# An attention and channel-mix kernel: the order of every engine, written out by hand before, made at trace time after

## The chip, the cores and the metric

The kernel runs on one core of one Trainium2 chip. The metric is the device time of one execution in microseconds (us). Before the change three runs gave 718.5, 718.63 and 719.32 us, with a median of 718.63 us.

## The reference

```python
# q, k, v: (8, 8, 576, 64);  x: (8, 576, 512);  w_k: (512, 1024), w_v: (1024, 512), w_r: (512, 512)
scores = scale * q @ k.T                       # scale = 1 / 8
mask   = (rel >= 0) & (rel < 64)               # rel = query position - key position
attn   = softmax(where(mask, scores, -1e9))    # divided by its sum + 1e-9
x      = (attn @ v), heads side by side        # (8, 576, 512)
x_prev = x shifted by one position, zero first
xk = mu_k * x + (1 - mu_k) * x_prev
xr = mu_r * x + (1 - mu_r) * x_prev
k  = maximum(xk @ w_k, 0)
v  = (k * k) @ w_v
r  = sigmoid(xr @ w_r)
out = r * v
```

A sliding-window attention over 64 positions feeds a channel-mix block: two mixes of each position with the one before it, three matrix products, a squared ReLU and a sigmoid gate.

## The kernel before

**Tiling of the attention.** The 576 positions of each batch and pair of heads are cut into 9 blocks of 64 queries; a block sees 128 keys. Eight blocks make a group, and there are 37 groups (the fifth holds four blocks). For one group TensorE (PE) writes the scores into two PSUM banks (`s`, one for each head of the pair; `scores`). For each half h of the group VectorE (DVE) adds the mask and takes the row's least value, four times (`pr`, `nmax`; in `soften`; the order lists it as ISA with a second row for `nmax`, and the profile as CUSTOM_DVE_ANT_0 with a READ_ACCUMULATOR). ScalarE (ACT) takes the exponential with the row's sum, four times. DVE makes the reciprocals (`rs`, `norm`), GpSimd (POOL) multiplies the four tiles by them (`pr<-pr,rs`), PE transposes them into one PSUM bank (`t`, `flip`), and ACT copies that bank out (`pt`, `keep`). With both halves there, PE multiplies with the values (`x`, `values`) and ACT copies the result into the transposed activations (`xT`, `keep_x`).

**Tiling of the channel mix.** The positions are cut into 11 units of 256, 320 and nine times 448 columns (`UNITS`). Every fp32 operand of the big products is split into a high and a low part in the fast fp32r format, so that each product takes three matmuls. For each unit DVE mixes (`d`, in `mix`), ACT rounds to the high part and POOL subtracts for the low part (`xk`, `xr`). Then PE does 96 matmuls with w_k, 48 with w_r and 96 with w_v. Each result tile of w_k goes through ACT (ReLU, `kf`), POOL (square), ACT (high part, `ks`) and DVE (low part, `ks<-kf,ks`); the w_r results go through ACT (`th`, `r`) and DVE; the w_v results are gated by DVE (`r<-m,r`, in the first unit `r<-mv,r`) and stored.

**Weights.** They come as 64-bit floats in 20 pieces of 128 x 512, four of w_r, eight of w_k and eight of w_v, and are decoded on the chip: ACT takes the absolute high word (`wt<-w`), DVE does four operations (`wt<-wt`, `wp<-wt`, `wp<-w,wp`, `wt<-w,wp`), ACT makes the high part (`ws`) and POOL the low part. All 20 are decoded before the first unit is through.

**What sets the order.** The wrapper class `Engine` keeps the compute instructions of each engine in the order in which the Python code issues them, so the order of the trace is the order on the engine; the transfers are issued by SyncE without it. That order is written by hand: a literal prologue for the first two groups, four weight pieces and the first mixes, and then a clock of steps. A step is six matmuls of the unit at work (`STEP = 6`, 40 steps to a unit). `BEGIN` lists the step at which each group's scores go to PE; `later(n, fn)` puts a follow-up n steps on; decodes stand two steps apart; the mixes for the next unit have fixed steps (20 to 39 of a unit). The transposes follow the scores by a number of steps worked out from the distance to the next group. In the first unit the w_v products run over the pieces of w_v in the outer loop, with two banks for all four results (`v_first`, tile `mv`); later units finish one result after another (`v_units`).

**Buffers around it.** `tmp` has five slots, shared by decode words, mixes, ReLU results and `th`; products and decodes share four PSUM banks (`m`); scores have two banks, `t` one, `x` one.

Of the kernel before, what the change touches and what calls it, by code (L numbers as in the profile page):

```python
# [9 lines left out]
F32 = mybir.dt.float32  # L10
# [6 lines left out]
P = 128  # L17
# [32 lines left out]
def attn_rwkv_kernel(ctx, tc, qT, kT, v2, mu_k, mu_r, w_k, w_v, w_r, out):  # L50
# [22 lines left out]
    pe, dve, sca, pool = (Engine(e) for e in (nc.tensor, nc.vector, nc.scalar, nc.gpsimd))  # L73
    now = 0
    due = {}
# [39 lines left out]
    raw = []  # L115

    def load_w(n):

        for ws, w, i, c in chunks[len(raw):len(raw) + n]:
            st = const.tile([P, WC, 2], U32, name="w", tag="w", bufs=len(chunks))  # L120
            nc.sync.dma_start(st.rearrange("p c t -> p (c t)"),
                              w[i * P:(i + 1) * P, c * WC:(c + 1) * WC].bitcast(U32))
            raw.append(st)
# [6 lines left out]
    def dec_abs(n):  # L130
        words[n] = tmp.tile([P, WC], F32, name="wt", tag="tmp", bufs=TB)
        sca.activation(words[n], raw[n][:, :, 1].bitcast(F32), AF.Abs)

    def dec_bits(n):
        lo, hi = raw[n][:, :, 0], raw[n][:, :, 1]
        tf = words[n]

        pt = ps_m.tile([P, WC], U32, name="wp", tag="m")
        dve.tensor_scalar(tf, tf, HI_MIN, HI_MAX, op0=ALU.max, op1=ALU.min)
        dve.tensor_scalar(pt, tf.bitcast(U32), 3, 0x3FFFFFF8,  # L140
                          op0=ALU.logical_shift_left, op1=ALU.bitwise_and)
        dve.scalar_tensor_tensor(pt, hi, 0xC0000000, pt, op0=ALU.bitwise_and, op1=ALU.bitwise_or)
        dve.scalar_tensor_tensor(tf.bitcast(U32), lo, 29, pt,
                                 op0=ALU.logical_shift_right, op1=ALU.bitwise_or)

    def dec_high(n):
        ws, _, i, c = chunks[n]
        ws[i, c] = const.tile([P, 2, WC], F32R, name="ws", tag="w", bufs=len(chunks))
        sca.copy(ws[i, c][:, 0], words[n])
# [436 lines left out]
```

## Time and profile before

| | before |
|---|---|
| median of 3 runs | 718.63 us |
| the profiled execution | 719.05 us |
| span of its profile (first to last instruction) | 716.8 us |
| PE busy | 650.5 us, 91% |
| DVE busy | 444.1 us, 62% |
| ACT busy | 367.2 us, 51% |
| POOL busy | 339.0 us, 47% |
| transfers | 56.5 MB, 79 GB/s over the span |

Times in the profile's rows are microseconds from the start of the span, but "mean ns" is in nanoseconds. A row of the timeline gives start, length, engine, line, operation, output and input tiles, shape and how many were merged; in brackets stands idle time before it and what ended that. A row of the stages table gives, for a stretch of the span, its length and then the busy time of each engine with the number of instructions, the TensorE clock granted, the busy share of the transfer engines and GB/s. All compute is recorded at one line, that of the wrapper (L71 before, L73 after), so groups are told apart by tiles.

### The profile page before, as it was taken

How to read it: one execution, taken by the hardware profiler on the slowest of the kernel's cores; microseconds unless marked ns; L12 is line 12 of the kernel's file. 1: busy time of each engine (PE TensorE's matmuls, PEld its weight loads, DVE VectorE, ACT ScalarE, POOL GpSimd, SP SyncE). 2: the span in 40 equal slices, each digit the busy share in tenths (PEclk: the TensorE clock that was granted, in tenths of full speed). 3: DMA queues.
4: the chain of work that ended last, by engine and by line, in shares of the span. 5: the costliest groups of instructions: out<-in, count | busy, mean ns of one | idle time of the engine just before them, and what ended most of it. 6: DMA issues, size and time to landing. Idle time of an engine off the chain costs nothing.

```text
span 716.8 us, 14398 instructions
## 1 busy us (share of the span) xinstructions
PE 650.5 (91%) x5232; PEld 584.0 (81%) x5232; DVE 444.1 (62%) x1372; ACT 367.2 (51%) x1111; POOL 339.0 (47%) x503
## 2 busy tenths in 40 slices
PE   4547665988999999999999999999999999999997
PEld 2446554887888988988889999988889898999997
DVE  4888887537636944873693584487368548638241
ACT  4556554555466446546635555645574563342330
POOL 4645464453743664454365375445436643424410
PEclk9857877999999999999999999999999999999999
DMA  8960220422221122233211022122221200101001
GB/s 253 339 246 32 88 70 0 156 64 72 91 94 63 60 89 64 76 109 101 81 53 58 14 83 89 63 77 102 70 88 60 89 1 15 39 1 38 14 1 52
DMA packets 33766, 56.50 MB, mean 79 GB/s; under 512 B 5024, under 2 KB 16800, under 8 KB 33696
## 3 DMA queue, kind: packets, MB, share of 16 engines
q1 hardware_dynamic: 33696, 55.59, 23.3%
q8 instruction: 41, 0.67, 0.4%
q14 instruction: 29, 0.24, 0.1%
HBM read 46.14 MB, written 9.44 MB: 78 GB/s over the span
## 4 chain that ended last, share of the span: by engine, by line
PE 74%; DVE 12%; ACT 6%; DMA 4%; issue 2%; SPq 1%; POOL 1%; ACTq 0%; POOLq 0%
PE m L71 59%; PE s L71 5%; PE x L71 4%; PE t L71 4%; DVE d L71 4%; DVE wp L71 3%; DVE wt L71 2%; ACT pr L71 2%; DMA v<-v 2%; DMA w<-w_v 1%; ACT wt L71 1%; DVE pr L71 1%; POOL pr L71 1%; PE mv L71 1%; DVE r L71 1%
## 5 line engine op out<-in xcount | busy, mean ns | idle before, releaser
L71 PE MATMUL m<-xk,ws 128*128 128x448 f32 (+2 forms) x1056 | 215.2, 358 | 4.8 <-POOL ws L71 2.4
L71 POOL TENSOR_SCALAR pr<-pr,rs 128x128 f32<-128x128 f32 x288 | 127.7, 461 | 189.1 <-DVE nmax L71 147.7
L71 PEld LDWEIGHTS m<-xk,ws 128*128 128x128 f32 x1056 | 188.3, 191 | 17.5 <-ACT ws L71 2.6
L71 PE MATMUL m<-ks,ws 128*128 128x448 f32 (+1 forms) x960 | 197.0, 361 | 0.0
L71 PEld LDWEIGHTS m<-ks,ws 128*128 128x128 f32 x960 | 174.4, 188 | 12.0
L71 DVE TENSOR_TENSOR ks<-kf,ks 128x448 fp32r<-128x448 f32 (+2 forms) x88 | 56.3, 640 | 125.9 <-ACT ks L71 125.9
L71 ACT ACTIVATE pr<-pr,nmax 128x128 f32<-128x128 f32 x288 | 112.9, 396 | 41.5 <-DVE nmax L71 41.4
L71 PE MATMUL m<-xr,ws 128*128 128x448 f32 (+2 forms) x528 | 114.5, 368 | 3.7 <-ACT xr L71 1.9
L71 POOL TENSOR_TENSOR kf<-kf 128x448 f32<-128x448 f32 (+2 forms) x88 | 77.9, 885 | 77.8 <-ACT kf L71 77.5
L71 PEld LDWEIGHTS m<-xr,ws 128*128 128x128 f32 x528 | 97.0, 198 | 11.4 <-POOL xr L71 2.7
L71 PE MATMUL t<-ident,pr 128*128 128x128 f32 x288 | 54.3, 302 | 41.4 <-ACT pt L71 26.3
L71 PEld LDWEIGHTS t<-ident,pr 128*128 128x128 f32 x288 | 37.7, 150 | 56.8 <-POOL pr L71 25.4
L71 ACT CAST ks<-kf 128x448 fp32r<-128x448 f32 (+2 forms) x88 | 47.5, 540 | 66.6 <-POOL kf L71 66.4
L71 DVE TENSOR_TENSOR d<-xT 128x256 f32<-128x256 f32 (+6 forms) x136 | 78.2, 575 | 0.1
L71 DVE CUSTOM_DVE_ANT_0 pr<-s,maskNone 128x128 f32<-128x128 f32 x224 | 55.2, 283 | 28.1 <-PE s L71 28.0
L71 POOL TENSOR_TENSOR xr<-d,xr 128x448 fp32r<-128x448 f32 (+2 forms) x44 | 51.2, 1170 | 32.0 <-ACT xr L71 31.7
L71 POOL TENSOR_TENSOR xk<-d,xk 128x448 fp32r<-128x448 f32 (+2 forms) x44 | 54.8, 1255 | 23.6 <-ACT xk L71 23.6
L71 ACT ACTIVATION_READ_ACCUMULATOR pr<-pr,nmax 128x1 f32 x288 | 54.9, 191 | 0.0
L71 ACT COPY xT<-x 128x256 f32<-128x256 f32 (+7 forms) x68 | 23.2, 391 | 59.7 <-PE x L71 59.6
L71 ACT COPY pt<-t 128x512 f32<-128x512 f32 (+1 forms) x74 | 42.2, 570 | 20.3 <-PE t L71 19.8
L71 PE MATMUL s<-k,q 64*64 64x128 f32 x1152 | 46.1, 302 | 5.9 <-DMA q<-qT 5.9
L71 DVE SCALAR_TENSOR_TENSOR d<-d,mur,xT 128x256 f32<-128x256 f32 (+6 forms) x68 | 49.1, 722 | 2.4
(44 smaller groups left out, 611.7 us busy)
## 6 DMA issues: line engine op xcount, KB each, us to landing
v<-v SPq DMA_DIRECT2D x56, 256.0 KB, 4.2
k<-kT SPq DMA_DIRECT2D x28, 288.0 KB, 2.8
q<-qT SPq DMA_DIRECT2D x28, 288.0 KB, 3.7
w<-w_k SPq DMA_DIRECT2D x8, 512.0 KB, 6.4
w<-w_v SPq DMA_DIRECT2D x8, 512.0 KB, 10.4
outT<-r SPq DMA_DIRECT2D x12, 224.0 KB, 1.9
w<-w_r SPq DMA_DIRECT2D x4, 512.0 KB, 4.6
outT<-r SPq DMA_DIRECT2D x12, 160.0 KB, 1.8
```

The lines of the kernel that those rows point to most:

```text
L71: return lambda *args, **kw: tc.keep_in_program_order(op(*args, **kw))
```

## The change

The clock of steps, `later`, `step`, the prologue and `at_step` go. Every piece of work becomes a `Piece` with an engine, a key (the step at which the hand-written order had it), an estimated length in ns, the pieces that it needs, and the buffers (`Hold`) that it takes or uses. `play` plays all pieces through on paper, when the kernel is traced: whenever an engine is free it takes, of its pieces whose inputs are there and whose buffers are free, the one with the lowest key. The list of pieces in the order in which they began is then traced, and as every engine keeps that order, so does the chip; the transfers are now kept in it too. A decode becomes seven pieces, so that other work may come between DVE's four operations. A product becomes pieces of three matmuls, so that several results may be open at once, and the first unit's w_v products now take the form of the later ones, with `spare=1` to leave a bank for the decodes. All eight maxima of a group may now precede the first reciprocals. The amount of work on every engine is unchanged, and so are the buffers, except that the small `sums` tiles have eight slots in place of four.

```diff
-BEGIN = (0, 6, 12, 18, 26, 34, 43, *range(53, 184, 10),
+BEGIN = (-30, -29, 0, 6, 12, 18, 26, 34, 43, *range(53, 184, 10),
          196, 210, 223, 236, 250, 263, 277, 286, 295, 304, 312, 322, 332, 342, 352)
+LINK = 50
...
-    def later(steps, fn, *args):
-        due.setdefault(now + steps, []).append((fn, args))
-
-    def step():
-        nonlocal now
-        now += 1
-        for fn, args in due.pop(now, ()):
-            fn(*args)
+    pe, dve, sca, pool, dma = (Engine(e) for e in (nc.tensor, nc.vector, nc.scalar, nc.gpsimd, nc.sync))
+    room = {"tmp": TB, "m": 4, "s": 2, "t": 1, "x": 1, "pr": 3, "sums": 4, "pt": 2, "xT": XB,
+            "ks": 8, "r": R_BUFS, "xr": 1, "xk": 1, "qk": 2, "v": 3}
...
+    def play():
+
+        left, free, now, begun = {}, {}, 0, []
+        for n, p in enumerate(pieces):
+            left.setdefault(p.engine, []).append((p.key, n, p))
+            free[p.engine] = 0
+        for e in left:
+            left[e].sort(key=lambda x: x[:2])
...
+            for e, ps in left.items():
+                if free[e] > now:
+                    continue
+                for i, (_, n, p) in enumerate(ps):
+                    if not all(q.done is not None and q.done + (q.lag if q.engine != e else 0) <= now
+                               for q in p.needs):
+                        continue
+                    tags = [h.tag for h in p.takes]
+                    if any(room[tag] < tags.count(tag) + p.spare for tag in set(tags)):
+                        continue
+                    del ps[i]
+                    for tag in tags:
+                        room[tag] -= 1
+                    free[e] = now + p.cost
+                    p.done = free[e]
+                    begun.append(p)
...
+    def over(n):
+
+        return 75 + 1.15 * n
...
+        p = Piece("ACT", key, 680, sign, [loaded], takes=[word])
+        p = Piece("DVE", key, 420, clamp, [p])
+        p = Piece("DVE", key, 700, shift, [p], takes=[bits])
+        p = Piece("DVE", key, 700, top, [p])
+        p = Piece("DVE", key, 690, low, [p], uses=[bits])
+        p0 = Piece("ACT", key, 630, first_part, [p])
+        decoded[id(ws), i, c] = p0, Piece("POOL", key, 1280, second_part, [p0], uses=[word])
...
+            q = Piece("DVE", key + 0.5, 375, least, [p, exps and softened or None],
+                      ([rows] if e == 0 else []), [bank])
+            softened = q
+            exps.append(Piece("ACT", key + 0.5, 590, exp, [q]))
...
+        q = Piece("DVE", key + 0.5, 350, shares, exps)
...
+            scaled.append(Piece("POOL", key + 0.5, 400, scale, [q]))
...
+        q = Piece("PE", key + 1, 110 * count, flip, scaled, [bank], [rows], lag=200)
+        q = Piece("ACT", key + 1, over(P * count), keep, [q], [kept], [bank])
...
+            needs = [last, *made[c], *decoded[id(w), c, col * P // WC]]
+            last = Piece("PE", key + 3 * c / STEP, 3 * (13 + n / 2.4), fn, needs,
+                         [bank] if c == 0 else [], uses(c), lag=200, spare=spare if c == 0 else 0)
...
+    DECODE = [-28 + 3 * n for n in range(4)] + [-10 + 2 * n for n in range(8)] + [8 + 2 * n for n in range(8)]
...
-    scores(0)
-    scores(1)
-    soften(0, 0, 0, 4)
-    dec_abs(0)
-    soften(0, 1, 0, 4)
-    dec_bits(0)
...
+    for p in play():
+        p.fn()
```

What this does to the order is shown at three places. In the rows, `s` are the scores, `t` the transposes, `x` the products with the values, `m` and `mv` the channel-mix products, `ws` the decoded weights.

The first place is VectorE at the start of the program, around the first decoded weight. Before:

```order
L71 ISA pr,nmax<-s,maskNone 128x128
L71 ISA nmax 128x1
L71 TENSOR_SCALAR wt<-wt 128x512
L71 TENSOR_SCALAR wp<-wt 128x512
L71 SCALAR_TENSOR_TENSOR wp<-w,wp 128x512
L71 SCALAR_TENSOR_TENSOR wt<-w,wp 128x512
L71 TENSOR_SCALAR rs<-sums 128x4
L71 RECIPROCAL rs<-rs 128x4
L71 ISA pr,nmax<-s,mask_101 128x128
```

The change:

```order
L73 ISA pr,nmax<-s,maskNone 128x128
L73 ISA nmax 128x1
L73 TENSOR_SCALAR rs<-sums 128x4
L73 RECIPROCAL rs<-rs 128x4
L73 TENSOR_SCALAR rs<-sums 128x4
L73 RECIPROCAL rs<-rs 128x4
L73 TENSOR_SCALAR wt<-wt 128x512
L73 TENSOR_SCALAR wp<-wt 128x512
L73 MEMSET xT 128x1 x2
L73 SCALAR_TENSOR_TENSOR wp<-w,wp 128x512
L73 SCALAR_TENSOR_TENSOR wt<-w,wp 128x512
```

The first decode stood after the eight maxima of group 0; now it stands after all sixteen maxima and all four reciprocal pairs of groups 0 and 1. From there on ten decodes follow one another with only mixes between them.

The second place is TensorE where the first unit (256 columns) ends and the second (320 columns) begins. Before:

```order
L71 MATMUL t<-ident,pr 128x128 x4
L71 MATMUL mv<-ks,ws 128x256 x12
L71 MATMUL s<-k,q 64x128 x16
L71 MATMUL x<-pt,v 64x64 x16
L71 MATMUL mv<-ks,ws 128x256 x30
L71 MATMUL t<-ident,pr 128x128 x4
L71 MATMUL mv<-ks,ws 128x256 x6
L71 MATMUL m<-xk,ws 128x320 x6
L71 MATMUL t<-ident,pr 128x128 x4
```

The change:

```order
L73 MATMUL m<-ks,ws 128x256 x36
L73 MATMUL m<-xk,ws 128x320 x6
L73 MATMUL t<-ident,pr 128x128 x4
L73 MATMUL m<-xk,ws 128x320 x12
L73 MATMUL t<-ident,pr 128x128 x4
L73 MATMUL m<-xk,ws 128x320 x9
L73 MATMUL s<-k,q 64x128 x16
L73 MATMUL x<-pt,v 64x64 x16
L73 MATMUL m<-ks,ws 128x256 x24
L73 MATMUL m<-xk,ws 128x320 x21
```

The scores shown are those of group 7 in both. Before, the second unit began when the first was through; now 27 of its matmuls stand ahead of the last 24 of the first unit.

The third place is TensorE further on, around the scores of one group at the end of the third unit (448 columns). Before:

```order
L71 MATMUL s<-k,q 64x128 x16
L71 MATMUL x<-pt,v 64x64 x16
L71 MATMUL m<-ks,ws 128x448 x36
L71 MATMUL t<-ident,pr 128x128 x4
L71 MATMUL m<-ks,ws 128x448 x6
L71 MATMUL m<-xk,ws 128x448 x6
L71 MATMUL t<-ident,pr 128x128 x4
L71 MATMUL m<-xk,ws 128x448 x12
```

The change:

```order
L73 MATMUL s<-k,q 64x128 x16
L73 MATMUL x<-pt,v 64x64 x16
L73 MATMUL m<-ks,ws 128x448 x24
L73 MATMUL m<-xk,ws 128x448 x3
L73 MATMUL t<-ident,pr 128x128 x4
L73 MATMUL m<-xk,ws 128x448 x12
L73 MATMUL t<-ident,pr 128x128 x4
L73 MATMUL m<-xk,ws 128x448 x6
```

The transposes of that group's first half moved from behind 36 product matmuls to behind 27; twelve still lie between the two halves.

More of the change, by code (lines that the diff above doesn't have):

```diff
@@ L202, in attn_rwkv_kernel @@
     banks, weights, sums, flipped = {}, {}, {}, {}
-    xTs, got = {}, set()
+    xTs, got = {}, {}
+    chain = {}
     def new_xT():
@@ L281, in keep_x @@
             sca.copy(xTs[n][:, 1 + i0 * W:1 + (i1 + 1) * W],
[L282 to L305 removed]
+                     flipped[t][:, o:o + i1 - i0 + 1].rearrange("p e r -> p (e r)"))
```

577 lines of the change are left out of this document (306 added, 271 removed).

## The prediction

> **What bounds the kernel now.** I read the page's first parts, then stages, then waits by stage. The page first:
>
> ```profile
> span 716.8 us, 14398 instructions
> ...
> PE   4547665988999999999999999999999999999997
> ...
> DVE  4888887537636944873693584487368548638241
> ...
> PEclk9857877999999999999999999999999999999999
> ```
>
> A slice is 17.9 us. For the first seven PE is half idle and DVE close to full; from about the eighth on PE is full and DVE has room. So there are two regimes. In the stages (the last three end with the last DVE row of group 7's softmax, with the second unit, and with the last matmul):
>
> ```profile
> 0.00:6.14 6.14, 2.27 (x32) 1.52 (x32) 0.00 (x0) 1.28 (x1) 3.97 (x19) 1.00 0.66 183
> 6.14:13.00 6.86, 2.85 (x35) 2.15 (x35) 5.67 (x32) 4.91 (x23) 1.18 (x4) 1.00 0.86 275
> 13.00:123.52 110.52, 65.59 (x572) 55.67 (x572) 89.81 (x232) 60.00 (x185) 59.32 (x89) 0.75 0.40 139
> 123.52:133.20 9.68, 9.62 (x110) 8.22 (x110) 7.62 (x28) 6.75 (x24) 5.67 (x8) 0.85 0.37 119
> 133.20:189.90 56.70, 51.01 (x528) 47.26 (x528) 32.31 (x125) 31.64 (x111) 27.21 (x46) 0.97 0.30 98
> 189.90:713.20 523.30, 519.21 (x3963) 469.13 (x3962) 308.08 (x958) 262.61 (x771) 241.65 (x339) 1.00 0.18 60
> ```
>
> Up to 133.2 us DVE works 5.67 + 89.81 + 7.62 = 103.1 us and stands still for 30.1. PE works 80.3 of the same 133.2, part of it at 0.75 of its clock. After 189.9 PE stands still for 4.1 us in 523, and the last 528 matmuls run at 105.82 / 528 = 0.200 us each without a break:
>
> ```profile
> 607.39 105.82 PE m L71 x528
> ```
>
> No order makes that part much shorter. What an order can shorten is the start, where DVE ends last, and there its waits count. What DVE and PE waited for up to 124 us (total, times, longest):
>
> ```profile
> DVE wt L71 <- ACT wt L71: 12.5, 16, 1.8
> DVE pr L71 <- PE s L71: 8.3, 4, 6.1
> DVE rs L71 <- ACT pr L71: 3.9, 5, 1.1
> ...
> PE t L71 <- ACT pt L71: 18.7, 6, 4.5
> PE t L71 <- POOL pr L71: 13.0, 7, 5.0
> ```
>
> The 12.5 us are no lack of data: sixteen times DVE reached a decode whose first step on ACT was queued behind something else. PE's 31.7 us at transposes follow from DVE being late with the softmax.
>
> **The change, part by part.** No operation is added or removed, so the whole sum is of waits.
>
> *First decode later.* On DVE it now follows both groups' softmax, and on ACT its first step follows all sixteen exponentials. The rows for that chain:
>
> ```profile
> 8.12 2.10 PE L71 MATMUL s<-k,q 64*64 64x128 f32 x32 [2.15 <-DMA q<-qT]
> 8.59 0.38 ACT L71 ACTIVATE pr<-pr,nmax 128x128 f32<-128x128 f32 x1
> 9.74 0.38 ACT L71 ACTIVATE pr<-pr,nmax 128x128 f32<-128x128 f32 x1
> L71 POOL TENSOR_SCALAR pr<-pr,rs 128x128 f32<-128x128 f32 x52 | 20.3, 409 | 30.7 <-DVE nmax L71 19.8 <-DVE rs L71 8.5 <-ACT ws L71 2.3
> L71 ACT COPY pt<-t 128x512 f32<-128x512 f32 (+1 forms) x74 | 42.2, 570 | 20.3 <-PE t L71 19.8
> L71 ACT ACTIVATE wt<-w 128x512 f32<-128x512 f32 x20 | 13.3, 665 | 0.0
> ```
>
> Group 1's scores end at 10.2. Then four maxima (0.9), the reciprocals of group 0's second half (0.35), its scaling on POOL (4 x 0.41), the transposes (about 0.5), the copy (0.57), four exponentials ((9.74 - 8.59) / 3 = 0.38 each, 1.5) and the decode's first step (0.67): 16.4 us. By then DVE has done 5.0 us (the 5.67 of the second stage less a decode of 2.5, plus four maxima and two pairs of reciprocals, 1.8). So it has stood still for 11.4 us by then, more than in the old order, which had its first decode under way at 8.71 us (row below).
>
> *The rest of the start.* From there the order holds something ready for DVE at nearly each place: ten decodes in a row, their first steps on ACT issued ahead. Up to the reciprocals of group 7 and the first unit's four gates (1.4) DVE has the same work as before, 103.1 + 1.4 = 104.5. It reaches that point at 16.4 + (104.5 - 5.0) = 115.9 plus what it still waits; before it was 133.2 + 1.4 = 134.6. The gain is 18.7 less those waits. They lie between 0 and 12.5 + (8.3 - 6.1) + 3.9 = 18.6, the 6.1 being the wait for the very first scores. I take 5: the 12.5 is a matter of queue places and mostly goes, the other two are of data and mostly stay. That makes 13.7 us.
>
> *Does PE follow?* What PE needs next are the second unit's xk and the end of the first unit:
>
> ```profile
> L71 DVE TENSOR_TENSOR ks<-kf,ks 128x256 fp32r<-128x256 f32 x8 | 7.0, 873 | 0.0
> L71 DVE TENSOR_TENSOR d<-xT 128x320 f32<-128x320 f32 x8 | 5.1, 632 | 0.0
> L71 DVE SCALAR_TENSOR_TENSOR d<-d,muk,xT 128x320 f32<-128x320 f32 x4 | 2.2, 552 | 0.1
> L71 DVE CUSTOM_DVE_ANT_0 pr<-s,maskNone 128x128 f32<-128x128 f32 x43 | 10.5, 283 | 1.4 <-PE s L71 1.4
> L71 DVE TENSOR_SCALAR wt<-wt 128x512 f32<-128x512 f32 x20 | 14.2, 712 | 12.5 <-ACT wt L71 12.5
> L71 DVE SCALAR_TENSOR_TENSOR wp<-w,wp 128x512 uint32<-128x512 uint32 x20 | 13.9, 696 | 0.7
> L71 DVE TENSOR_SCALAR wp<-wt 128x512 uint32<-128x512 uint32 x20 | 13.9, 695 | 0.7
> L71 DVE SCALAR_TENSOR_TENSOR wt<-w,wp 128x512 uint32<-128x512 uint32 x20 | 13.7, 686 | 0.7
> 122.91 0.69 DVE L71 SCALAR_TENSOR_TENSOR wt<-w,wp 128x512 uint32<-128x512 uint32 x1
> 133.14 1.04 PE L71 MATMUL m<-xk,ws 128*128 128x320 f32 x6
> 139.17 5.47 PE m L71 x36
> ```
>
> The last decode ended at 123.6. In the new order four mixes (1.2 each), eight maxima (0.28), two pairs of reciprocals (0.35) and two `ks` (0.87) that stood ahead of it stand behind it, 9.5 us; so it ends at 16.4 + (95.5 - 9.5 - 5.0) + 4 of waits = 101. Behind it come five mixes, eight maxima, two `ks`, two pairs of reciprocals and a gate, 11 us, before the last xk of unit two; ACT and POOL add 1.5. PE then has 18 matmuls of 320 columns (5.47 / 36 = 0.15 each), a set of transposes, a score burst with its values (2.1) and the last 24 of 256 columns (0.12): 8 us. That is 122 us, with 27 matmuls of unit two done. Before, unit two began at 133.1 and had 27 done, by the same pace, 4 us later, at 137. The two counts give 14 and 15; I keep 13.7.
>
> Here a rule speaks against the change. On DVE the `wt<-wt` operation takes 0.43 us at its shortest but 0.71 in the mean above, and one `ks` took 2.96:
>
> ```profile
> 8.71 0.43 DVE L71 TENSOR_SCALAR wt<-wt 128x512 f32<-128x512 f32 x1 [0.79 <-ACT wt L71]
> 93.75 2.96 DVE L71 TENSOR_TENSOR ks<-kf,ks 128x256 fp32r<-128x256 f32 x1
> ```
>
> The Trainium skill, page "GPSIMD Engine Reference", section "8. Key points", says that GpSimd shares its SBUF interfaces with VectorE and contends with those VectorE instructions that run in a two-port mode or read two SBUF inputs. The trace agrees as far as it goes: 0.71 against 0.43. What more of this would cost stands among the rivals.
>
> *The second unit.* In 133.2 to 189.9 PE stands still for 5.7 us, at transposes that follow the scores closely. The new order has 39 to 48 matmuls ahead of a group's first transposes there, rather than 36, and unit two has a start. I take 3 of the 5.7, between 0 and 5.7.
>
> *The later units.* There the transposes move closer to the scores. For one group before (PE, then the two halves' scaling on POOL):
>
> ```profile
> 242.35 1.10 PE L71 MATMUL s<-k,q 64*64 64x128 f32 x32
> 243.39 1.15 PE L71 MATMUL x<-pt,v 128*64 128x64 f32 x32
> ...
> 251.79 0.60 PE L71 MATMUL t<-ident,pr 128*128 128x128 f32 x4
> ...
> 248.86 1.41 POOL L71 TENSOR_SCALAR pr<-pr,rs 128x128 f32<-128x128 f32 x4 [0.81 <-DVE rs L71]
> ...
> 253.14 2.09 POOL L71 TENSOR_SCALAR pr<-pr,rs 128x128 f32<-128x128 f32 x4 [1.60 <-DVE d L71]
> ```
>
> Four transposes take 0.4 to 0.6 us, the second value being their row's. Half 0 was scaled 7.9 us after the scores began, half 1 12.9. In the new order the transposes stand 2.1 + 27 x 0.2 = 7.5 and 7.5 + 0.4 + 12 x 0.2 = 10.3 us after them. With the old chain PE would wait for both. But the maxima of both halves now come in one go, so that half 1's exponentials need not wait for a DVE round behind mixes: 3 us for values and copy, 8 x 0.38 for exponentials, 0.4 for reciprocals, 1.7 for POOL behind half 0 make about 8.5 to 9.8, just within the place. I take 0, between a gain of the 4.1 us that PE still loses there and the loss in the second rival.
>
> Sum: 13.7 + 3 + 0 = 16.7. The profiled execution took 719.05 us, 2.25 outside its span and 0.4 above the median of 718.63. The span would be 716.8 - 16.7 = 700.1, the time 702.4 against the profiled one, 702 against the median.
>
> **The rivals.**
>
> *More: 690.* DVE hardly waits in the start (18.7), unit two loses its 5.7, and the later units their 4.1: 28.5 us, 718.6 - 28.5 = 690. For it: all three come from one cause, waits by queue place. Against it: the planner counts 420 ns for the `wt<-wt` operation that takes 712 here, so that its order is made for a DVE that never collides. 18%.
>
> *Slower: 734.* The fixed place of the transposes. If the chain of half 1 keeps its 12.9 us, PE waits 12.9 - 10.3 = 2.6 for a group, and there are 25 groups after 190 us; already half of that, 1.3 x 25 = 32, gives 702 + 32 = 734. It decides from 0.7 us per group on. For it: the 7.9 and 12.9 above. Against it: DVE and ACT have room there (308 and 263 of 523) and the order of the maxima has changed. 9%.
>
> *No gain: 715 to 720.* DVE's two-input operations meet POOL more often as both are packed. In the start these are 20 `wt<-wt` (0.28 over the shortest), some 18 halves of mixes and eight `ks` (0.45 over), about 13 us of stretch in all; were it twice that, the 13.7 would be gone: 716. Against it: most of a decode's time goes to the three operations with PSUM at one end, whose means (695, 696 and 686 ns) lie close together, without a stretch. That the planner's estimates are so far off that its order means nothing on the chip ends here too. 12%.
>
> **How the numbers follow.** The forecast's own range is 692 to 713 (61%). The bounds of the terms give 690 to 719. With the rivals 8 in 10 lie in 686 to 717. A difference of under 0.2% (1.4 us) can't be told from no change here. Faster by over 0.2%: the forecast 61, more 18, and over half of the no-gain case, 86% together; within 0.2%: 4%; slower: 10%.
>
> **What would show it.** DVE's first `wt<-wt` near 16.4 us; its waits for `wt` from ACT under 3 us in the start; the last `wt<-w,wp` near 101; the last matmul of 256 columns near 122; PE still for under 4 us in unit two; the last matmul near 696.5. I'm wrong if the last decode ends after 115, or if PE's waits for `pr` or `pt` at transposes after 190 us pass 10 us.

## The result, and the profile after

| | before | after |
|---|---|---|
| median | 718.98 us (718.5 to 723.53, 4 runs) | 690.69 us (689.68 to 691.39, 4 runs) |
| ratio | 1 | 0.9592, interval 0.955 to 0.9634 |
| profiled execution | 719.05 us | 691.39 us |
| span | 716.8 us | 689.6 us |

The change saves 28.3 us by the medians and 27.2 by the spans; 16.7 was forecast. The page after, first parts, and then the stages up to the last decode, the end of the first unit, the end of the second and the last matmul:

```profile
span 689.6 us, 14350 instructions
...
PE   5657888999999999999999999999999999999997
...
DVE  2998985485487269447926824883595478177241
...
PEclk9756799999999999999999999999999999999999
```

```profile
0.00:17.00 17.00, 9.95 (x105) 7.11 (x106) 4.83 (x41) 9.39 (x36) 8.21 (x31) 1.00 0.81 254
17.00:96.90 79.90, 56.23 (x448) 47.41 (x451) 73.25 (x193) 51.26 (x148) 49.88 (x67) 0.70 0.48 169
96.90:118.40 21.50, 19.08 (x224) 17.05 (x218) 15.23 (x57) 12.40 (x45) 15.04 (x19) 0.92 0.29 94
118.40:159.45 41.05, 40.98 (x431) 39.45 (x430) 28.99 (x104) 26.82 (x95) 25.20 (x39) 1.00 0.31 97
159.45:686.20 526.75, 524.00 (x4037) 472.51 (x4036) 305.66 (x980) 266.91 (x791) 255.12 (x349) 1.00 0.19 62
```

PE is fuller in six of the first seven slices (the fourth is equal), and full from the eighth on without the dip that before had in the ninth and tenth; in the second unit (118.4 to 159.45 us) it stands still for 0.07 us. Three places of the timeline bound the stages, DVE's first and last decode operations and PE's last 256-column matmuls with what follows:

```profile
17.00 0.43 DVE L73 TENSOR_SCALAR wt<-wt 128x512 f32<-128x512 f32 x1 [0.17 <-ACT wt L73]
...
96.20 0.69 DVE L73 SCALAR_TENSOR_TENSOR wt<-w,wp 128x512 uint32<-128x512 uint32 x1
```

```profile
115.34 3.10 PE L73 MATMUL m<-ks,ws 128*128 128x256 f32 x24
118.28 3.24 PE L73 MATMUL m<-xk,ws 128*128 128x320 f32 x21
...
159.43 0.78 PE L73 MATMUL m<-xk,ws 128*128 128x448 f32 x3
...
666.34 19.37 PE L73 MATMUL m<-ks,ws 128*128 128x448 f32 x96
```

Where the 27.5 us between the ends of the last products (713.2 and 685.7) come from, by equal work on PE. Before, PE had the first unit, the scores of group 7 and 27 matmuls of the second unit done at 138.4 (18 of them when group 8's scores began at 136.98, nine more at 0.15 us); after, at 118.3. That is 20.1 us. But before, both sets of group 7's transposes were through at that mark, and after they were not; a set takes 0.36 us of PE, so by equal work it is 19.4 us. The second unit then ended at 190.2 before, with four score bursts (2.1 us each with their values) and seven sets of transposes in the stretch, and at 159.4 after, with three and six. So 51.8 - 2.5 - 41.1 = 8.2 us come from the second unit. The rest took 523.0 us before; after it took 526.3 with one burst and three sets more, 3.2 us, so 523.1: -0.1.

What DVE waited for up to the last decodes and gates (124 us):

```profile
DVE pr L73 <- PE s L73: 12.0, 4, 7.0
DVE rs L73 <- ACT pr L73: 6.8, 6, 2.3
DVE r L73 <- PE m L73: 2.3, 1, 2.3
DVE d L73 <- POOL ws L73: 0.6, 1, 0.6
DVE wt L73 <- ACT wt L73: 0.3, 2, 0.2
```

The sixteen waits of 12.5 us for a decode's first step are gone. But this is not the whole of it. Up to the end of group 7's reciprocals and the first gates, 295 DVE instructions in both kernels, the stages say (before, then after):

```profile
0.00:134.60 134.60, 81.73 (x752) 68.57 (x752) 104.50 (x295) 73.03 (x231) 71.24 (x123) 0.78 0.43 146
```

```profile
0.00:119.60 119.60, 86.46 (x776) 72.77 (x777) 94.34 (x295) 74.26 (x233) 73.33 (x117) 0.79 0.49 167
```

Of the 15.0 us, 10.2 are less busy time of DVE (104.50 to 94.34) and only 4.8 less standing still (30.1 to 25.3). Of the 10.2, 8.1 are shorter instructions (the lengths of the 295 add up to 117.7 us before and 109.7 after); in the other 2.1 an instruction begins before the one ahead of it has ended. Of the 8.1 us, 6.1 are in two operations with SBUF at both ends, most of the rest in the mixes:

```profile
L73 DVE TENSOR_TENSOR ks<-kf,ks 128x256 fp32r<-128x256 f32 x8 | 4.5, 561 | 0.0
...
L73 DVE TENSOR_SCALAR wt<-wt 128x512 f32<-128x512 f32 x20 | 10.6, 532 | 0.3 <-ACT wt L73 0.3
```

They had 873 and 712 ns in the mean before. The three operations of a decode with PSUM at one end are as they were (694, 693 and 684 ns). POOL became slower: a scaling up to 124 us took 465 ns in the mean, 409 before.

### The profile page after: what moved, and what is told of

Read it like the earlier page. It is cut to its first block, busy times and chain, and to the rows that moved or that the text cites. A ratio compares the mean times of both kernels' runs of the same rounds, so it can differ in the third digit from the quotient of the medians.

```text
span 689.6 us, 14350 instructions
## 1 busy us (share of the span) xinstructions
PE 650.2 (94%) x5232; PEld 583.5 (85%) x5232; DVE 428.1 (62%) x1372; ACT 366.8 (53%) x1111; POOL 353.4 (51%) x503
## 4 chain that ended last, share of the span: by engine, by line
PE 81%; DVE 7%; POOL 4%; DMA 3%; issue 2%; ACT 2%; SPq 1%; POOLq 0%; ACTq 0%
PE m L73 68%; PE x L73 5%; PE s L73 4%; PE t L73 4%; POOL pr L73 2%; DVE wp L73 2%; DVE d L73 2%; DVE wt L73 2%; POOL ws L73 1%; DMA w<-w_k 1%; DMA k<-kT 1%; ACT pr L73 1%; SPq L73 1%; DMA v<-v 1%; DVE r L73 1%
## 5 line engine op out<-in xcount | busy, mean ns | idle before, releaser
L73 PE MATMUL m<-xk,ws 128*128 128x448 f32 (+2 forms) x1056 | 223.9, 365 | 5.1 <-ACT xk L73 1.8
L73 POOL TENSOR_SCALAR pr<-pr,rs 128x128 f32<-128x128 f32 x288 | 139.1, 500 | 146.8 <-DVE rs L73 124.4
L73 PE MATMUL m<-ks,ws 128*128 128x448 f32 (+2 forms) x1056 | 212.8, 357 | 0.0
L73 PEld LDWEIGHTS m<-xk,ws 128*128 128x128 f32 x1056 | 192.0, 195 | 21.1 <-POOL xk L73 2.2
L73 PEld LDWEIGHTS m<-ks,ws 128*128 128x128 f32 x1056 | 187.4, 190 | 13.2
L73 DVE TENSOR_TENSOR ks<-kf,ks 128x448 fp32r<-128x448 f32 (+2 forms) x88 | 62.9, 729 | 125.6 <-ACT ks L73 125.6
L73 PE MATMUL m<-xr,ws 128*128 128x448 f32 (+2 forms) x528 | 114.0, 368 | 13.1 <-ACT r L73 6.2
L73 ACT ACTIVATE kf<-m 128x448 f32<-128x448 f32 (+2 forms) x88 | 44.8, 519 | 38.8 <-PE m L73 38.2
L73 ACT CAST ks<-kf 128x448 fp32r<-128x448 f32 (+2 forms) x88 | 46.1, 542 | 30.7 <-POOL kf L73 30.6
L73 PE MATMUL t<-ident,pr 128*128 128x128 f32 x288 | 52.1, 297 | 10.7 <-POOL pr L73 10.4
L73 DVE SCALAR_TENSOR_TENSOR r<-m,r 128x448 f32<-128x448 f32 (+2 forms) x44 | 25.9, 589 | 58.2 <-PE m L73 58.2
L73 PE MATMUL s<-k,q 64*64 64x128 f32 x1152 | 44.2, 291 | 6.0 <-DMA q<-qT 4.5
```

The source lines that it names most:

```text
L73: return lambda *args, **kw: tc.keep_in_program_order(op(*args, **kw))
```

## The experiments

The main theory is that the start is shorter since a decode's first step on ACT is issued ahead ("queue places"); the first rival is that the order on PE did it.

**The old kernel with the first step issued ahead.**

```diff
     def decode(n):
-        dec_abs(n)
+        if n == NC:
+            dec_abs(n)
         later(1, dec_bits, n)
+        if n + 1 < len(chunks):
+            later(1, dec_abs, n + 1)
```

> The kernel before, with one thing altered: from the fifth weight piece on, the first step of a decode on ACT (wt<-w) is issued one step earlier, ahead of the high part (ws) of the decode before it. In the old order ACT takes that high part first, which waits for DVE's last operation of the decode before, so DVE stands still for 0.63 + 0.67 us at a decode (the 12.5 us of 16 waits). Theory 'queue places': DVE's waits for wt up to 124 us fall from 12.5 to under 4 us, the last decode ends 8 to 12 us earlier than at 123.6, and the time falls by 8 to 12 us, to 707 to 711. Rival 'PE's order': what made the start shorter is the order on PE (several results open, the second unit begun early, transposes elsewhere); DVE then waits for scores in place of wt, and the time falls by under 3 us. A side question: before, wt<-wt took 712 ns in the mean, and after 532. If that is because POOL's low part of the decode before ran beside it (both were released by the same high part), the mean falls to some 530 here as well; if it has to do with something else, it stays near 700.

713.59 us (712.86 to 714.89), ratio 0.9913 with 0.9894 to 0.9932: 6 us less, between the two. The last decode ended 5.5 us earlier, and every mark behind it came 5.5 us earlier too, up to the last matmul: what DVE gains in the start reaches the end undiminished. Up to the last decode DVE stood still for 21.9 us, 28.0 before, but its work rose by 0.7. DVE's waits of this run up to 124 us (total, times, longest), and its group of wt<-wt:

```profile
DVE pr L71 <- PE s L71: 9.1, 3, 6.8
DVE wt L71 <- ACT wt L71: 5.2, 5, 1.8
```

```profile
L71 DVE TENSOR_SCALAR wt<-wt 128x512 f32<-128x512 f32 x20 | 16.0, 798 | 5.2 <-ACT wt L71 5.2
```

7.3 us of waits went; wt<-wt became longer, not shorter. The answer to the side question is "no" for this kernel: the first step comes ahead, but DVE still reaches wt<-wt while POOL's subtraction runs. So in the old kernel queue places alone account for a good quarter of the 19.4 us that PE gains in the start.

**The changed kernel without the head start of the second unit.**

```diff
-            needs = [last, *made[c], *decoded[id(w), c, col * P // WC]]
+            needs = [last, closed[0] if c == 0 else None, *made[c], *decoded[id(w), c, col * P // WC]]
...
         v_units(base + 24, u, k2, gate, n)
+        closed[0] = final[0] if u == 0 else None
```

Here `final[u]` is the last piece of the unit's last product with w_v.

> The changed kernel, with the second unit held back: its products with w_k may not begin until the first unit's last product with w_v is through, as in the old order. Theory 'the head start fills waits': 27 matmuls of 320 columns at 0.15 us, 4.0 us, have nothing to stand in for them at the end of the first unit, where PE would wait for weights and ks; the time rises by 2.5 to 4 us, to 693 to 695. Rival 'no place for it': in 96.9 to 119.6 us PE stands still for only 2.4 us in the changed kernel, and the first unit's own work is enough to keep it busy; the 4.0 us are only done later, in time that is lost anyway; the time changes by under 1 us.

689.87 us (689.48 to 690.38), ratio 0.9582 with 0.9566 to 0.9597: the same as the changed kernel. The 27 matmuls done early are worth nothing; both kernels begin the third unit within 0.7 us of each other (158.8 and 159.4). One part of the rival on PE falls with this.

**The same, and the first step not issued ahead.**

```diff
-        p = Piece("ACT", key, 680, sign, [loaded], takes=[word])
+        p = Piece("ACT", key, 680, sign, [loaded, rounded.get(n - 1)], takes=[word])
...
-        p0 = Piece("ACT", key, 630, first_part, [p])
+        p0 = rounded[n] = Piece("ACT", key, 630, first_part, [p])
```

> The run with the second unit held back, and with a decode's first step on ACT allowed only when the high part of the decode before is through, as in the old order; all else is still ordered by the planner. To be compared with the run that only holds the second unit back. Theory 'queue places': up to 0.63 + 0.67 us at each of 19 decodes, less what mixes and softmax fill, come back: DVE's waits for wt are 5 to 14 us, the last decode ends 6 to 12 us later and the time is 6 to 12 us longer. Rival 'PE's order': under 2 us longer. Side question: if POOL's low part beside it stretches wt<-wt, its mean goes back from 532 to some 700 ns, and POOL's scaling (pr<-pr,rs, 465 ns in the mean up to 124 us) falls towards the 409 of before.

705.73 us (705.16 to 706.3), 15.9 more than with the first step ahead; the interval of its ratio, 0.9785 to 0.9818, lies far from that of the other. More than the theory had, and for a second reason. DVE's waits of this run up to 124 us, and the group:

```profile
DVE pr L73 <- PE s L73: 11.5, 3, 7.1
DVE wt L73 <- ACT wt L73: 6.4, 10, 1.5
```

```profile
L73 DVE TENSOR_SCALAR wt<-wt 128x512 f32<-128x512 f32 x20 | 16.7, 834 | 6.5 <-ACT wt L73 6.4
```

The last decode ended at 117.2 in place of 96.5 us. Of these 20.8 us, 6.1 are waits for wt and 7.4 are wt<-wt (834 ns in place of 467). The remaining 7.3 aren't split: the planner also put other work ahead of the last decode (201 DVE instructions in place of 193 in the stage). The side question has half a yes: wt<-wt went back up, but POOL's scaling up to 124 us did not fall towards the 409 ns of before. It took 502 ns, against 461 in the run with the second unit held back. So what DVE saves in such meetings is not simply what POOL pays.

**POOL's low part cut down, in the old kernel.** How the two engines meet can be read in the timeline of before:

```profile
64.87 1.28 POOL L71 TENSOR_TENSOR ws<-wt,ws 128x512 fp32r<-128x512 f32 x1 [1.16 <-ACT ws L71]
...
65.40 1.04 DVE L71 TENSOR_SCALAR wt<-wt 128x512 f32<-128x512 f32 x1 [0.45 <-ACT wt L71]
...
69.40 1.28 POOL L71 TENSOR_TENSOR ws<-wt,ws 128x512 fp32r<-128x512 f32 x1 [2.49 <-ACT ws L71]
...
69.95 1.01 DVE L71 TENSOR_SCALAR wt<-wt 128x512 f32<-128x512 f32 x1 [0.24 <-ACT wt L71]
```

POOL's subtractions end at 66.15 and 70.68, the DVE operations that began beside them at 66.44 and 70.96: 0.28 to 0.29 us later each time, whatever was left of the subtraction. It is no slower pace but a wait for the other's end.

```diff
-        pool.tensor_sub(ws[i, c][:, 1], words.pop(n), ws[i, c][:, 0].bitcast(F32))
+        o = 64
+        pool.memset(ws[i, c][:, 1, o:].bitcast(F32), 0.0)
+        pool.tensor_sub(ws[i, c][:, 1, :o], words.pop(n)[:, :o], ws[i, c][:, 0, :o].bitcast(F32))
```

> The kernel before, with 7/8 of each decode's low part left out: POOL sets 448 of 512 columns to zero and subtracts only in the other 64 (so that most of the weights have no low part). It takes away most of the time in which POOL holds a subtraction of 512 columns. In the trace of before a wt<-wt that begins while POOL runs such a subtraction lasts until 0.28 us after its end (1.01 to 1.56 us in place of 0.43, 8 of 20 times). Theory 'one waits for the other': the mean of wt<-wt falls from 712 to 430 to 480 ns, 4.6 to 5.6 us less of DVE in the start, and as DVE ends last there, the last decode comes earlier than at 123.6 and the time falls by 3 to 6 us. Rival 'waits fill it': the first step of the next decode on ACT still stands behind the high part, DVE's waits for wt rise from 12.5 us by what the stretch gives back, and the time changes by under 1 us.

713.4 us (711.03 to 716.29), ratio 0.9912 with 0.9884 to 0.994. The group of wt<-wt in this run, and the stage up to its last decode:

```profile
L71 DVE TENSOR_SCALAR wt<-wt 128x512 f32<-128x512 f32 x20 | 9.4, 468 | 11.4 <-ACT wt L71 11.4
```

```profile
0.00:117.00 117.00, 70.47 (x635) 58.94 (x636) 88.43 (x264) 66.15 (x207) 54.68 (x130) 0.79 0.46 157
```

Before, the same 264 DVE instructions took 95.6 us of work and ended at 123.6. Now it is 7.1 us less work, 0.5 more standing still, and the last decode comes 6.6 us earlier. The theory holds, a little above its size: meeting POOL's low parts cost the old start about 7 us, and DVE's waits did not fill it.

**DVE's four operations of a decode as one piece.**

```diff
-        p = Piece("DVE", key, 420, clamp, [p])
-        p = Piece("DVE", key, 700, shift, [p], takes=[bits])
-        p = Piece("DVE", key, 700, top, [p])
-        p = Piece("DVE", key, 690, low, [p], uses=[bits])
+        p = Piece("DVE", key, 2510, four, [p], takes=[bits])
```

> The changed kernel, with DVE's four operations of a decode as one piece of the planner (2510 ns), so that no other work may come between them, as in the old order. Theory 'fine pieces matter': maxima and mixes wait up to 2.5 us behind a decode, PE gets its transposes later in the start, and the time rises by 2 to 6 us. Rival 'what matters is what is issued ahead': DVE is the engine that ends last in the start and has something ready either way; the time changes by under 1.5 us.

698.81 us (697.37 to 699.77), ratio 0.9712 with 0.9691 to 0.9732: 8.1 more than the changed kernel, above what the theory had. The stage of this run from the first decode to the last:

```profile
17.00:96.60 79.60, 46.10 (x385) 37.71 (x385) 76.08 (x168) 47.01 (x125) 45.35 (x57) 0.70 0.44 154
```

The last decode is where it was (96.6 us), but the softmax and mixes stood behind decodes: DVE did 168 instructions rather than 193, PE 385 rather than 448 in 46.1 us rather than 56.2. PE then did that work later. So in the start DVE's end is not all; what PE gets while the decodes run counts as well. wt<-wt rose to 756 ns here.

**The second unit.** PE's waits at transposes in the second unit of before, 5.6 us, all stood at half 1. By what ended them, most waited for the copy on ACT:

```profile
PE t L71 <- ACT pt L71: 4.3, 3, 2.2
PE t L71 <- POOL pr L71: 1.3, 2, 0.8
```

First half 1's softmax was issued earlier in the old kernel, then, in another run, the copy of the transposes:

```diff
-            if period < 9:
+            if period < 9 or 7 <= t <= 11:
```

> The kernel before, with one thing altered in groups 7 to 11 (the end of the first unit and the second): the four maxima and the exponentials of half 1 are issued one to two steps earlier, behind those of half 0, and its reciprocals and scaling two steps earlier, as groups that stand close together have it. The places of the transposes on PE stay. Theory 'half 1 is late': PE's waits at transposes in the second unit (1.84, 2.17, 0.26, 0.84 and 0.47 us, 5.6 in all) all stand at half 1, whose softmax is issued in the fourth and fifth steps behind the scores; they go almost wholly, and with them the lower clock behind them (12 matmuls took 2.87 us where others take 1.76); the second unit takes 5 to 8 us less and so does the whole, 711 to 714. Rival 'the places on PE': half 1's place is too early for any order on DVE and ACT; the waits stay over 3 us and the time falls by under 2 us.

```diff
-            later(f + 1, keep, t, h)
+            later(f + (t not in range(7, 12)), keep, t, h)
```

> The kernel before, with one thing altered in groups 7 to 11: the copy of the transposes out of PSUM on ACT (pt<-t) is issued in the same step as the transposes, not in the next. PE's places and the softmax stay. In the trace of before, the transposes of a half 0 ended at 145.1 us, but their copy began at 147.96: on ACT it stood behind two ks casts, which waited for POOL's squares, and these stood behind the scaling of half 1. Half 1's transposes need the bank that the copy gives back, and waited 1.84 us. With the softmax of half 1 issued earlier that wait did not go (2.68 us), as the copy stayed behind the casts. Theory 'queue place of the copy': PE's waits at transposes from 134 to 190 us fall from 5.6 to under 1.5 us, the lower clock behind them goes too, and the second unit takes 4.5 to 8 us less; the time is 711.5 to 715. Rival 'the copy holds up the rest': ACT now stands still in front of the copy until PE has transposed, so the ks casts come later, PE waits for ks, and the time changes by under 1.5 us.

The first gave 720.31 us (719.36 to 725.16, ratio 1.0024 with 1.0003 to 1.0045), no gain; PE's waits at transposes from 134 to 192 us were 7.6 in its profile, that of the slowest of its ten runs. The second gave 715.2 (714.73 to 716.23, ratio 0.994 with 0.9916 to 0.9964), 4.5 us less. The timeline of before shows why, from half 0's transposes to half 1's:

```profile
144.48 0.60 PE L71 MATMUL t<-ident,pr 128*128 128x128 f32 x4
144.50 0.46 ACT L71 CAST ks<-kf 128x320 fp32r<-128x320 f32 x1 [0.45 <-POOL kf L71]
...
144.91 1.64 POOL L71 TENSOR_SCALAR pr<-pr,rs 128x128 f32<-128x128 f32 x4 [0.43 <-PE t L71]
...
146.52 0.72 POOL L71 TENSOR_TENSOR kf<-kf 128x320 f32<-128x320 f32 x1
147.27 0.46 ACT L71 CAST ks<-kf 128x320 fp32r<-128x320 f32 x1 [1.97 <-POOL kf L71]
...
147.96 0.58 ACT L71 COPY pt<-t 128x512 f32<-128x512 f32 x1
...
148.68 0.63 PE L71 MATMUL t<-ident,pr 128*128 128x128 f32 x4 [1.84 <-ACT pt L71]
```

The transposes were over at 145.1; ACT stood still for 1.97 us in front of a ks cast, that cast waited for POOL's square, and the square stood behind the scaling of half 1. Only then came the copy that gives the one bank back. In the changed kernel the copy began 0.03 us after the transposes (133.97, then 134.00). With the copy moved in the old kernel, the stretch from the last 256-column matmuls to the third unit took 53.7 us, not 57.8, and 1.9 us of waits were left, all in one group's half 1 (171 to 173.5 us). Theory "queue place of the copy" holds in its mechanism and falls just short of each of its bounds: 1.9 us of waits, not under 1.5; 4.1 us less, not 4.5 to 8; 715.2 us, not 715. Its claim on the clock failed. Before, the clock granted to TensorE fell to a half soon after the wait of 2.17 us (163.03):

```profile
164.00:167.30 3.30, 3.30 (x26) 2.97 (x28) 1.70 (x6) 1.04 (x3) 0.00 (x0) 0.50 0.00 0
```

```profile
163.41 3.12 PE L71 MATMUL m<-xr,ws 128*128 128x320 f32 x12
166.46 1.51 PE L71 MATMUL s<-k,q 64*64 64x128 f32 x32
```

The 12 matmuls took 3.12 us where others took 2.00, and the scores 1.51 where others took 1.10: 1.5 us. With the copy moved, such a stretch is still there, behind the waits that are left (0.50 from 173.8 to 177.0 us). In the changed kernel the clock is 1.00 in all of the second unit.

**How thin the places of the transposes are.**

```diff
-            exps.append(Piece("ACT", key + 0.5, 590, exp, [q]))
+            exps.append(Piece("ACT", key + 0.5, 385, exp, [q]))
```

> The changed kernel, with one estimate of the planner altered: an exponential counts 385 ns, as the traces have it (0.38 us), in place of 590. It brings the planned transposes nearer to the scores: at the end of the fourth unit half 1 stands 6 matmuls behind half 0 rather than 12, 1.2 us earlier. In the changed kernel's trace half 0's scaling ended 1.25 us ahead of its transposes and half 1's 0.8 us (group whose scores began at 218.05 us). Theory 'thin margin' (the slower rival of the prediction): PE waits 0.4 to 1 us for a group at half 1, 10 to 25 us over the 25 groups after 160 us, and the time rises to 700 to 715. Rival 'the chain moves along': DVE, ACT and POOL are given the new order too, do half 1 earlier, and PE's waits stay under 5 us; the time changes by under 2 us.

710.58 us (709.98 to 712.38), ratio 0.9883 with 0.9859 to 0.9907: 20 us longer, with the estimate that is nearer to the chip. The theory's time came, mostly at another place. The start has another order altogether: DVE's first decode operation begins at 9.35 us, not 17.00. PE's waits at transposes in this run, up to 158 us and from there:

```profile
PE t L73 <- POOL pr L73: 17.4, 14, 9.2
```

```profile
PE t L73 <- POOL pr L73: 7.2, 14, 1.3
```

In the later units the waits are 7.2 us, 2.2 in the changed kernel, far from 10 to 25. The larger loss is in the start: one wait of 9.2 us, and the last 256-column matmul at 128.3 us, not 118.3. Behind the start of the third unit another 8.4 us are lost; 5.0 are those waits, 2.3 are a slower pace of the last 528 matmuls in this profile (last section), and 1.1 isn't attributed.

Then three estimates were made longer, on the kernel with the second unit held back:

```diff
-        p = Piece("DVE", key, 420, clamp, [p])
+        p = Piece("DVE", key, 530, clamp, [p])
...
-        decoded[id(ws), i, c] = p0, Piece("POOL", key, 1280, second_part, [p0], uses=[word])
+        decoded[id(ws), i, c] = p0, Piece("POOL", key, 1320, second_part, [p0], uses=[word])
...
-            scaled.append(Piece("POOL", key + 0.5, 400, scale, [q]))
+            scaled.append(Piece("POOL", key + 0.5, 500, scale, [q]))
```

> The run with the second unit held back (689.9 us), and with three estimates of the planner set to what the traces show where DVE and POOL meet: wt<-wt 530 in place of 420 ns, POOL's low part of a decode 1320 in place of 1280, one scaling 500 in place of 400. Theory 'longer estimates are safe': transposes are planned up to 0.4 us later behind POOL, so that PE's waits for pr (11.0 us up to 124 us) shrink; the time falls by 0 to 3 us. Rival 'any change of an estimate makes another order': the start comes out by chance, as with the exponential's estimate (20 us longer) and the decode in one piece (8 us longer), and the time changes by over 4 us, either way.

690.37 us (689.21 to 691.37): no difference that can be told. The first theory's fall of 0 to 3 us is met at best at its lower end, and its reason is wrong: PE's waits for pr up to 118 us rose to 17.4 us. The last decode ended at 98.6 us, 2.1 later than in the kernel that this one was made from, without a price in the time. The rival's large swing did not come either.

**Using DVE's idle start.** DVE stood still for 12.2 of its first 17.0 us. Three orders of the decodes were tried, by their keys. Two first, in the changed kernel:

```diff
-    DECODE = [-28 + 3 * n for n in range(4)] + [-10 + 2 * n for n in range(8)] + [8 + 2 * n for n in range(8)]
+    DECODE = [-40, -40] + [-28 + 3 * n for n in range(2, 4)] + [-10 + 2 * n for n in range(8)] + [8 + 2 * n for n in range(8)]
```

> The changed kernel, with the first two decodes put ahead of the softmax of groups 0 and 1 in the planner's keys. DVE's first wt<-wt was at 17.0 us, with 4.8 us of work done by then. Theory 'the first decode comes too late': two decodes of 2.5 us fit into those waits, DVE's first wt<-wt is at 9 to 11 us, the last decode ends 3 to 5 us earlier than at 96.9, and the time falls by 2.5 to 5 us, to 686 to 688. Rival 'the softmax is the longer chain': groups 0 and 1 are scaled and transposed up to 5 us later, the first unit's mixes with them, and PE begins its products later; the time changes by under 1 us or rises.

All four of w_r first, with the second unit held back:

```diff
-    DECODE = [-28 + 3 * n for n in range(4)] + [-10 + 2 * n for n in range(8)] + [8 + 2 * n for n in range(8)]
+    DECODE = [-40] * 4 + [-10 + 2 * n for n in range(8)] + [8 + 2 * n for n in range(8)]
```

> The run with the second unit held back (689.9 us), and with the first four decodes, all of w_r, ahead of the softmax of groups 0 and 1. With the first two alone put ahead, DVE's first wt<-wt came at 8.4 us in place of 17.0, but PE waited 9.7 us for a later piece of w_r, the last decode ended 2.2 us later and the time rose by 2.5 us. Theory 'all of w_r or none': PE's first products need all four pieces; with all four first, the wait goes, the early 12 us of DVE are used, and the time falls by 2 to 5 us, to 685 to 688. Rival 'DVE's time at the start is not what is short': PE cannot begin its products before the mixes, which stand behind the softmax; PE's wait only changes its name, and the time is the same within 1.4 us or longer.

The same, with the other sixteen spread out:

```diff
-    DECODE = [-40] * 4 + [-10 + 2 * n for n in range(8)] + [8 + 2 * n for n in range(8)]
+    DECODE = [-40] * 4 + [-3 + 2 * n for n in range(8)] + [13 + 2 * n for n in range(8)]
```

> The run with the second unit held back and the first four decodes first (684.7 us), with the keys of the other sixteen decodes raised: the fifth to twelfth by 7 steps, the last eight by 5, so that decodes and the softmax of groups 3 and 4 take turns on DVE. In that run PE waited 9.3 us at one set of transposes (at 51.31 us): the maxima behind them stood on DVE behind five decodes in a row (36 to 48 us). Theory 'PE stands still there for nothing': the wait falls to under 4 us, PE has more of its first unit done while the decodes go on, and the time falls by 2 to 4 us, to 681 to 683. Rival 'DVE sets the end of the start': what comes earlier on DVE puts the decodes later by as much, PE waits for weights or ks in place of pr, and the time stays within 1.4 us or rises.

Two first: 693.24 us (691.68 to 693.78, ratio 0.9621 with 0.9599 to 0.9642), 2.5 more, as its rival had it. PE waited 9.7 us for wt, and wt<-wt was back at 697 ns. Four first: 684.74 us (684.34 to 685.51), ratio 0.9518 with 0.9492 to 0.9544, 5.1 less than without; this is just below the range of its theory, and the fastest kernel of the study. Four, spread out: 690.75 us (690.47 to 692.03, ratio 0.9582 with 0.9566 to 0.9598), 6.0 more than that, again as its rival had it. DVE's last decode operation with four first, and PE's waits at transposes up to 118 us:

```profile
90.22 0.69 DVE L73 SCALAR_TENSOR_TENSOR wt<-w,wp 128x512 uint32<-128x512 uint32 x1
```

```profile
PE t L73 <- POOL pr L73: 19.3, 13, 9.3
```

The same two rows spread out (waits up to 124 us):

```profile
99.02 0.69 DVE L73 SCALAR_TENSOR_TENSOR wt<-w,wp 128x512 uint32<-128x512 uint32 x1
```

```profile
PE t L73 <- POOL pr L73: 12.8, 12, 2.5
```

With four first the last decode comes 5.6 us earlier than in the kernel it was made from (96.5), the third unit begins 5.6 earlier, and the gain is at the end almost whole, although PE once waits 9.3 us. Spread out, that wait shrinks to 2.5 us as its theory said, yet the last decode comes 8.8 us later and the time is 6.0 longer. Here PE's longest wait was no loss; the last decode was the mark to watch. From its end to the start of the third unit, 62.3 to 62.5 us pass in the changed kernel, in the one with the second unit held back, and in these three. It is no rule: 56.9 us pass without the first step ahead, 60.8 with the longer estimates, 68.4 with a decode as one piece, and 72.3 with the shorter exponential.

## Why the prediction came out as it did

The direction was right. The time, 690.69 us, lies 1.3 us below the forecast's own range (692 to 713) and inside the wider one that the rivals make (686 to 717). The sum was 10.5 us short on the span, 16.7 against 27.2, and two of its terms were mis-sized: the start (13.7, measured 19.4 at PE) and the second unit (3, measured 8.2).

*First decode later.* Forecast 16.4 us, DVE still for 11.4; measured 17.00 and 12.2. Right. That it cost something is shown by the run with four decodes first.

*The rest of the start.* DVE was to be through group 7 at 120.9 us, and was at 119.6. This is two errors that cancel. Remaining waits were put at 5 us and are 25.3 - 12.2 = 13.1: the waits for wt went as said (12.5 to 0.3), those for scores and exponentials did not merely stay but grew, from 6.1 us (without the very first scores) to 11.8. And "DVE has the same work as before" failed: as many instructions kept DVE busy for 10.2 us less, 8.1 of them by their own lengths. The failing step is the one that held instruction lengths fixed under a new order. The run with the cut-down low part puts a price on them, 7.1 us in the old start, and the run without the first step ahead shows that the order makes them: 467 to 834 ns for wt<-wt. How the 19.4 us split among the parts of the change stays open: the first step ahead was worth 6.1 us in the old order and 15.9 in the new, the finer pieces of a decode 8.1, and such shares overlap.

*Does PE follow?* Last decode 101 forecast, 96.9 measured: first decode +0.6, work of the stage 73.25 in place of 81 (-7.75), standing still 6.65 in place of 4 (+2.65). Last 256-column matmul 122 forecast, 118.3 measured. So the gain at PE was 19.4 us, not 13.7 to 15: 3.7 us more by this mark, 1.4 as the 137 of before was itself early by the rows, less 0.7 for the transposes of group 7, which the count left out. The head start of the second unit, which the count used, plays no part: without it the time is the same. The run with the decode in one piece shows what PE does need besides the last decode, its softmax and mixes in time.

*The rule.* The page "GPSIMD Engine Reference" of the Trainium skill, section "8. Key points", was weighed as a price to come on top, in the no-gain rival. The effect exists and its sign was the other way: the new order has fewer such meetings on DVE. Operations wt<-wt that took over 0.8 us: 8 of 20 before, 3 of 20 after. That POOL's longer scaling (409 to 465 ns) is the other side of this is not shown. The Trainium skill's page "SBUF — State Buffer", section "SBUF: two separate sides", says that the pair of ports is locked for a whole instruction, and that the later one waits for its end. The rows of before agree, with 0.28 to 0.29 us from POOL's end to DVE's.

*The second unit.* 3 us forecast, 8.2 measured, over the upper bound of 5.7. The cause named, transposes close behind the scores, was wrong for most of it: for 4.3 of the 5.6 us half 1 waited for a bank whose copy stood in ACT's queue. The run that moved half 1's softmax gained nothing; the one that moved the copy took 4.1 us off the unit. The bound failed as it counted standing still alone. Behind a wait PE also worked at half its clock (0.50 from 164.0 to 167.3 us), which cost 1.5 us. With the 5.6 us of waits that makes 7.1 of the 8.2; the other 1.1 wasn't measured by itself.

*The later units.* 0 forecast, -0.1 measured, with 2.2 us of waits at transposes, 3.7 before. Right, but by less than a microsecond: in one group (scores at 218.05 us) the scaling of half 0 ended 1.25 us and that of half 1 0.8 us ahead of the transposes, and the run with the shorter exponential lost 5 us there.

*The rivals.* The time of "More", 690, came, but not its account: DVE did not "hardly wait", the later units gave nothing back, and shorter instructions, the larger part of DVE's 15.0 us, were in no case, so that the time fits it by luck. "Slower" did not come; its mechanism is there in the exponential's run, but at 5.0 us and not 32. "No gain" had the right mechanism with the wrong sign.

## What to carry to other kernels

When an order changes, ask not only which waits go but which instructions will run beside which: the durations read from the old trace belong to the old neighbours. To find what a start is bound by, follow the last operation of its longest chain (here the last decode) before the longest wait, and check that what comes behind it keeps its length; here it did in some orders and not in others. In a planner, any estimate that is altered makes another order: making one truer cost 20 of the 28 us here, of which 5.0 are shown to be lost margin in the later units and most of the rest came from another start; making three longer gained nothing.

## What the runs showed of the hardware that was not expected

DVE's wt<-wt, from SBUF to SBUF, when it begins while POOL runs a subtraction of 512 columns, ends 0.28 to 0.30 us after the subtraction, whatever is left of that; begun 0.03 us ahead of one (at 23.30 us in the changed kernel) it keeps its 0.42 us. The order alone sets how often this happens: its mean was 467 ns in one order of the changed kernel and 834 in another.

The clock granted to TensorE fell to a half for more than 3 us in the midst of a full stretch, behind a wait of 2.17 us in one run and behind three of 0.61, 0.84 and 0.47 us in another. A wait of 1.84 us (148.68 us, before) had no such stretch behind it. So a wait can cost more than its length, and which ones do was not found out.

The pace of the last products differs between profiles at the same granted clock of 1.00: 96 matmuls took 19.36 to 19.37 us in most kernels, 19.79 in the one with the shorter exponential, and 20.00 in the profiles of the cut-down low part and of the earlier half 1, 3.5 us over the last 528. So the stages of such profiles were compared, not their ends. Its cause stays open.
